# Softmax attention and a leaky-ReLU layer on one core: row 8 of batch 0 is loaded and attended later, batch 1's q comes in two loads

## The chip, the cores and the metric

The kernel runs on one core of a Trainium2 chip. The metric is the device time of one execution in microseconds (us). TensorE is called PE, VectorE DVE, ScalarE ACT, GpSimd POOL and SyncE SP, as in the profile. Each has its own queue of instructions, which it works off in order; data that one engine makes for another is handed over by semaphores.

## The reference

Inputs are q, k, v of 8 batches x 8 heads x 576 rows x 64, and two weight matrices, all fp32. Per head, q is softmaxed along its 64 columns and k along its 576 rows; then q times (k transposed times v). The result, 4608 tokens of 512, goes through two matrix products with a leaky ReLU between them.

```python
q_s = softmax(q, axis=-1)
k_s = softmax(k, axis=2)
kv = np.einsum('bhsd,bhse->bhde', k_s, v)
x = np.einsum('bhsd,bhde->bhse', q_s, kv)      # then to (4608, 512)
h = x @ w_in                                    # w_in: 512 x 2048
out = np.maximum(0.01 * h, h) @ w_out           # w_out: 2048 x 512
```

## The kernel before

The schedule is written out by hand: the order in which the program emits instructions is the order of each engine's queue. A framework adds semaphores and gives out buffers: a tile taken from a pool whose buffers are all in use waits until an older one is released.

A batch lies in SBUF as 128 partitions x 4 head pairs x 9 rows x 64 columns. A "row" r of a batch below means one of these nine, 64 tokens of each head. The output of attention for all batches is xT (bf16, transposed), and the two layers run over it in nine tiles of 512 tokens. Since a batch has 576 tokens, tile 0 is batch 0's rows 0 to 7, and tile 1 is batch 0's row 8 and batch 1's rows 0 to 6.

Attention of some rows takes these steps. `load` (L80, SP) fetches q, k or v. For q: `q_max` (L214, DVE), `q_sub` (L273, POOL or DVE), `q_exp` (L281, ACT), `q_sum` (L290 and L292, DVE), `q_norm` (L297, DVE), `q_transpose` (L402, PE, into PSUM) and `q_keep` (L417 or L419, a copy out of PSUM). For k: `k_tree` (L150), `k_allmax` (L155 to L175), `k_sub` (L183), `k_exp` (L191, ACT). `v_cast` (L201 on ACT, L203 on POOL) makes bf16 of v. `kv` (L310, PE) multiplies k and v into two PSUM tiles, `kd_make` (L329, L330) divides by k's sums, `cross` (L429, PE) applies q, and `x_keep` (L452, L454) copies the result to xT. Batch 0 has special forms of some steps (`q_first`, `kv_pair`, `k_max_pe`).

PSUM has two pools: psB with six buffers of 2 KB per partition and psO with two. In layer 2 of tile 0 (L499) the four accumulators `pout` take the two of psO and two of psB.

Tile 0 is cut into halves of 256 tokens. For half 0, layer 1 (`begin`, `end_pe`, L478) runs in two groups of eight column blocks, J0 and J1, and between its passes it does attention work of batch 0 (`x1`, `t2`, `x2`). Then comes half 1, and then layer 2 in 16 steps of four matmuls. J1 needs the second half of w_in.

Work of batch 1 hangs on hooks: `at(t, u, ...)` places functions at point u of tile t, and `run(t, u)` emits them. In tile 0, points 16 to 31 follow the 16 blocks of half 1 (two at a time, after the leaky ReLU of a pair), and point 32 + j follows step j of layer 2. So point 41 comes after 40 layer-2 matmuls, and point 45 after 56.

Loads go through two queues. SP's queue carries q, k, v and the stores; POOL's carries the weights, which it casts to bf16 on the way (`load_w_in`, `load_w_out`). `hold_sync` makes SP wait: the first one waits for a block of w_in's second half, and behind it SP issues batch 1's k in two parts, q's rows 0 to 6, and v. The second one, in `late_loads`, waits for a block of w_out and is followed by the rest of batch 1's q and by batch 2. POOL waits in the same way for the last block of w_in (L601) before it issues w_out's other blocks.

Of the kernel before, what the change touches and what calls it, by code (L numbers as in the profile page):

```python
# [8 lines left out]
FP32 = mybir.dt.float32  # L9
# [10 lines left out]
L = 64  # L20
# [5 lines left out]
def kernel(  # L26
# [9 lines left out]
    nc = tc.nc  # L36
# [10 lines left out]
    P = 128  # L47
    NB = C // P
    NF = F // P
    TT = 512  # L50
# [18 lines left out]
    BANK_TAG = "bank2k"  # L69


    def load(src, b, name, cuts, t=None):

        if t is None:
            t = raw_pool.tile([P, HL, R, D], FP32, name=name, tag="raw")
        flat = src[b].rearrange("h s d -> (h s d)").rearrange(
            "(hl p r d) -> p hl r d", hl=HL, p=P, r=R
        )
        for hs, rs in cuts:
            nc.sync.dma_start(  # L80
                out=t[:, hs, rs].rearrange("p h r d -> p h (r d)"),
                in_=flat[:, hs, rs].rearrange("p h r d -> p h (r d)"),
            )
        return t

    ALLH, ALLR = slice(0, HL), slice(0, R)
# [5 lines left out]
    st[0]["q"] = load(q, 0, "q_raw", [(ALLH, RA)])  # L92
    st[0]["k"] = load(k, 0, "k_raw", [(slice(0, 2), ALLR), (slice(2, 4), ALLR)])
    st[0]["v"] = load(v, 0, "v_raw", [(slice(0, 2), ALLR), (slice(2, 4), ALLR)])
    load(q, 0, "q_raw", [(ALLH, RB)], st[0]["q"])

    zero = const_pool.tile([P, TT], BF16)
    nc.gpsimd.memset(zero, 0.0)  # L98
# [91 lines left out]
    def k_exp(b, hs):  # L190
        nc.scalar.activation(  # L191
            out=st[b]["ke"][:, :, hs].rearrange("p r h d -> p h r d"),
            in_=st[b]["k"][:, hs],
            func=AF.Exp,
        )

    def v_cast(eng, b, gg):
        o = vb2[b % 2][:, :, gg, :, 0:D].rearrange("p r h d -> p h r d")
        i = st[b]["v"][:, 2 * gg : 2 * gg + 2]
        if eng is nc.scalar:  # L200
            eng.copy(out=o, in_=i)  # L201
        else:
            eng.tensor_copy(out=o, in_=i)  # L203
# [7 lines left out]
    def q_max(b, rs):  # L211
        n = rs.stop - rs.start
        st[b]["qmax", rs.start] = m = small_pool.tile([P, HL, n], FP32, name="qmax")
        nc.vector.tensor_reduce(out=m, in_=st[b]["q"][:, :, rs], axis=AX.X, op=ALU.max)  # L214
# [55 lines left out]
    def q_sub(eng, b, rs):  # L270
        n = rs.stop - rs.start
        qs = st[b]["q"][:, :, rs]
        eng.tensor_tensor(  # L273
            out=qs,
            in0=qs,
            in1=st[b]["qmax", rs.start].unsqueeze(3).to_broadcast([P, HL, n, D]),
            op=ALU.subtract,
        )
# [119 lines left out]
    def q_transpose(b, r0, n, pool=psB_pool, tag=BANK_TAG):  # L398
        ps = pool.tile([P, NB, n, L], BF16, name="psum_qt", tag=tag)
        for rr in range(n):  # L400
            for gg in range(2):
                nc.tensor.matmul(  # L402
                    ps[:, gg::2, rr],
                    lhsT=st[b]["qe"][:, r0 + rr, 2 * gg : 2 * gg + 2].rearrange(
                        "p h d -> p (h d)"
                    ),
                    rhs=ident,
                    is_transpose=True,
                    start=(rr == 0 and gg == 0),
                    stop=(rr == n - 1 and gg == 1),  # L410
                )
        st[b]["ps", r0] = ps

    def q_keep(eng, b, r0, n, gs=slice(0, 4)):
        o, i = st[b]["qT"][:, gs, r0 : r0 + n], st[b]["ps", r0][:, gs]
        if eng is nc.scalar:
            eng.copy(out=o, in_=i)  # L417
        else:
            eng.tensor_copy(out=o, in_=i)  # L419
# [44 lines left out]
    def attend_all(b, *parts):  # L464
        for fn in sum([attend_rows(b, *p) for p in parts], []):
            fn()

    def q_turn(b, rs=ALLR):
        if rs.start == 0:
            st[b]["qX"] = qT_pool.tile([P, R * 2, P], BF16, name="qX", tag="qT")  # L470
        nc.sync.dma_start_transpose(
            out=st[b]["qX"][:, 2 * rs.start : 2 * rs.stop],
            in_=st[b]["qe"][:, rs].rearrange("p r h d -> p (r h d)"),
        )
# [35 lines left out]
    def at(t, u, *fns):  # L510
        while t > 0 and u >= 32:
            t, u = t + 1, u - 32
        hooks.setdefault((t, u), []).extend(fns)
# [15 lines left out]
    def hold_sync(i, src):  # L529
        nc.sync.dma_start(out=held[:, i], in_=src)  # L530
# [59 lines left out]


    hold_sync(0, w_in_sb[0:1, 0, F - 128 : F])
    st[1]["k"] = load(k, 1, "k_raw", [(H0, ALLR), (H1, ALLR)])
    RM, RE = slice(4, 7), slice(7, R)
    st[1]["q"] = load(q, 1, "q_raw", [(ALLH, slice(0, 7))])
    st[1]["v"] = load(v, 1, "v_raw", [(ALLH, ALLR)])

    def late_loads():
        q_max(0, R3)
        q_sub(nc.gpsimd, 0, R3)  # L600
        nc.gpsimd.tensor_copy(out=gate[:, 0:1], in_=w_in_sb[:, NB - 1, F - 1 : F])  # L601
        for j0, j1 in ((2, 4), (4, 6), (6, 8), (8, 10), (10, 12), (12, 16)):
            load_w_out(slice(j0, j1))
        hold_sync(1, w_out_sb[0:1, 11, 0:128])
        load(q, 1, "q_raw", [(ALLH, RE)], st[1]["q"])
        load_all(2)


    at(0, 22, lambda: q_transpose(0, 8, 1), lambda: q_keep(nc.scalar, 0, 8, 1))
    at(0, 26, lambda: attend_all(0, (R3, (nc.scalar, nc.vector))))  # L610
    at(0, 20, lambda: k_begin(1), lambda: q_begin(1), lambda: k_tree(1, H0), lambda: k_tree(1, H1))
    at(0, 20, lambda: q_max(1, RA), lambda: q_sub(nc.gpsimd, 1, RA), lambda: k_allmax(1))
    at(0, 20, lambda: k_sub(nc.vector, 1, H1), lambda: k_sub(nc.gpsimd, 1, H0))
    at(0, 20, lambda: q_max(1, RM), lambda: q_sub(nc.gpsimd, 1, RM), lambda: v_cast(nc.gpsimd, 1, 1))
    at(0, 31, lambda: q_exp(1, RA), lambda: q_sum(1, RA), lambda: q_norm(1, RA))
    at(0, 31, lambda: k_exp(1, H1), lambda: v_cast(nc.scalar, 1, 0), lambda: k_exp(1, H0))
    at(0, 32, lambda: q_exp(1, RM), lambda: q_sum(1, RM), lambda: q_norm(1, RM))
    for r0 in (0, 2):
        at(0, 41, lambda r0=r0: q_transpose(1, r0, 2), lambda r0=r0: q_keep(nc.scalar, 1, r0, 2))
    at(0, 41, lambda: kv(1), lambda: kd_make(1))  # L620
    at(0, 44, lambda: q_transpose(1, 4, 3), lambda: q_keep(nc.scalar, 1, 4, 3))
    at(0, 45, lambda: attend_all(1, (slice(0, 7), (nc.scalar, nc.vector))))
    at(0, 46, lambda: q_max(1, RE), lambda: q_sub(nc.gpsimd, 1, RE), lambda: q_exp(1, RE))
    at(1, 14, lambda: q_sum(1, RE), lambda: q_norm(1, RE))
    at(1, 25, lambda: q_transpose(1, 7, 2), lambda: q_keep(nc.scalar, 1, 7, 2))
# [63 lines left out]
    def end_act(j, ph, half):  # L689
# [4 lines left out]
    t2 = (  # L694
        lambda: q_transpose(0, 6, 2, psO_pool, "pout"),
        lambda: q_keep(nc.vector, 0, 6, 2),
        lambda: q_sum(0, R3),
    )
    x2 = (
        lambda: attend_all(0, (slice(4, 8), (nc.scalar, nc.vector))),  # L700
        lambda: q_norm(0, R3),
    )
    x1 = (
        lambda: attend(0, (1,), RA),
# [6 lines left out]
    begun = list(zip(J0, begin(J0, ((0, x1), (1, ()), (2, ())))))  # L711
    for j, ph in begun:
        end_pe(j, ph, 0, slice(3, 4), False)
    for i, (j, ph) in enumerate(begun):
        end_act(j, ph, 0)
        if i == 0:
            q_sum(0, R1)
            q_norm(0, R1)
            q_exp(0, R2)
            late_loads()  # L720
            q_sum(0, R2)
            q_norm(0, R2)
        if i == 1:
            q_transpose(0, 4, 2, psO_pool, "pout")
            q_keep(nc.scalar, 0, 4, 2)
    q_exp(0, R3)
    for j, ph in zip(J1, begin(J1, ((0, t2), (1, x2), (2, ())))):
        end_pe(j, ph, 0, slice(3, 4), False)
        end_act(j, ph, 0)
# [69 lines left out]
```

## Time and profile before

| | us |
|---|---|
| median of 3 runs | 285.56 (285.51 to 285.58) |
| the profiled execution | 285.4 |
| its span in the profile | 283.6 |
| PE busy | 275.2 (97%) |
| ACT busy | 146.1 (52%) |
| DVE busy | 141.5 (50%) |
| POOL busy | 89.7 (32%) |
| DMA, mean over the span | 162 GB/s |

Times inside the execution count from the start of the span. A line of a timeline has the start, the duration, the engine, the source line, the operation with its tiles and shapes, and how many instructions are merged into it; in brackets is the idle time of the engine before it, and what ended that. A line of the waits has who waited for whom, the total, how often, and the longest. A line on DMA issues ends with the size and the time from issue to landing.

### The profile page before, as it was taken

The numbers are of one execution on the slowest core, as the hardware profiler recorded it, in microseconds if no ns is written. First come the engines' busy times: TensorE is split into PE (matmuls) and PEld (weight loads), VectorE is DVE, ScalarE is ACT, GpSimd is POOL, SyncE is SP. The second block draws the span as 40 slices with busy tenths as digits, with TensorE's granted clock in tenths as the row PEclk, the third lists the DMA queues.
The fourth block names the chain that finished last, engine by engine and source line by source line (L and its number), as shares of the span: only waits on it lengthen the run. The fifth ranks groups of instructions, "written<-read, shape, count | busy, mean of one in ns | idle before, by whom it ended". The sixth has DMA issues, their size and how long they took to land.

```text
span 283.6 us, 4991 instructions
## 1 busy us (share of the span) xinstructions
PE 275.2 (97%) x2022; PEld 132.8 (47%) x2022; DVE 141.5 (50%) x237; ACT 146.1 (52%) x260; POOL 89.7 (32%) x63
## 2 busy tenths in 40 slices
PE   7789999999999999999999999999999999999995
PEld 3368644444444544444444444444444444444443
DVE  2975695977870993497093718481711100110011
ACT  4976573775359426921973367435843165016400
POOL 2956390035069019407800690059000000000000
PEclk9999999999999999999999999999999999999999
DMA  7999999894659175953498339832052210230033
GB/s 239 334 211 341 281 177 395 265 352 159 152 122 404 51 161 132 408 121 75 102 401 158 74 80 378 201 76 63 11 86 55 61 34 0 55 82 14 0 74 76
DMA packets 37143, 45.81 MB, mean 162 GB/s; under 512 B 16000, under 2 KB 20352, under 8 KB 37120
## 3 DMA queue, kind: packets, MB, share of 16 engines
q1 hardware_dynamic: 33648, 41.16, 48.9%
q0 software_dynamic: 3312, 4.20, 8.4%
q8 instruction: 16, 0.26, 0.4%
q10 hardware_dynamic: 160, 0.13, 0.1%
q14 instruction: 7, 0.06, 0.1%
HBM read 36.70 MB, written 9.44 MB: 163 GB/s over the span
## 4 chain that ended last, share of the span: by engine, by line
PE 77%; DMA 8%; DVE 8%; POOL 3%; issue 1%; SPq 1%; ACT 0%; DVEq 0%; POOLq 0%
PE pout L499 39%; PE ph L478 34%; DMA q_raw<-in_q_dram 3%; DMA w_in_sb<-in_moe_w_in_dram 3%; DMA k_raw<-in_k_dram 2%; PE pkv L310 2%; PE po L429 2%; DVE qmax L214 2%; DVE k_raw L183 1%; POOL q_raw L273 1%; DVE out_sb L493 1%; DVE qe L297 1%; DVE t L150 1%; POOL w_in_sb L123 1%; SPq L80 1%
## 5 line engine op out<-in xcount | busy, mean ns | idle before, releaser
L499 PE MATMUL pout<-w_out_sb,gj 128*128 128x512 bf16 (+2 forms) x592 | 128.1, 373 | 0.0
L478 PE MATMUL ph<-xT,w_in_sb 128*128 128x512 bf16 (+1 forms) x640 | 127.4, 358 | 0.7 <-DMA w_in_sb<-in_moe_w_in_dram 0.7
L487 ACT ACTIVATE gj<-ph 128x512 bf16<-128x512 f32 x144 | 81.7, 602 | 54.1 <-PE ph L478 53.5
L478 PEld LDWEIGHTS <-w_in_sb 128*128 128x128 bf16 x640 | 61.9, 98 | 62.3 <-DMA w_in_sb<-in_moe_w_in_dram 0.8
L499 PEld LDWEIGHTS <-gj 128*128 128x128 bf16 x592 | 56.2, 98 | 65.2 <-ACT gj L487 0.7
L493 DVE COPY out_sb<-pout 128x512 f32<-128x512 f32 (+1 forms) x34 | 22.7, 676 | 88.2 <-PE pout L499 82.7
L183 POOL TENSOR_TENSOR k_raw<-k_raw,kall 128x2304 f32<-128x2304 f32 (+1 forms) x6 | 29.1, 4857 | 75.6 <-DVE kall L175 62.1
L452 ACT CAST xT<-po 128x512 bf16<-128x512 f32 (+4 forms) x46 | 18.2, 486 | 43.6 <-PE po L429 43.6
L273 POOL TENSOR_TENSOR q_raw<-q_raw,qmax 128x2304 f32<-128x2304 f32 (+5 forms) x13 | 31.6, 2431 | 24.3 <-DVE qmax L214 23.6
L290 DVE TENSOR_REDUCE qsum<-qe 128x36 f32<-128x2304 bf16 (+5 forms) x13 | 20.1, 1544 | 33.0 <-ACT qe L281 33.0
L297 DVE TENSOR_TENSOR qe<-qe,qrec 128x2304 bf16<-128x2304 bf16 (+5 forms) x13 | 21.5, 1650 | 0.4
L214 DVE TENSOR_REDUCE qmax<-q_raw 128x36 f32<-128x2304 f32 (+5 forms) x13 | 19.9, 1538 | 1.9 <-DMA q_raw<-in_q_dram 1.9
L191 ACT ACTIVATE ke<-k_raw 128x2304 bf16<-128x2304 f32 (+2 forms) x11 | 17.6, 1603 | 5.8 <-POOL k_raw L183 4.5
L281 ACT ACTIVATE qe<-q_raw 128x2304 bf16<-128x2304 f32 (+5 forms) x13 | 17.2, 1324 | 4.7 <-POOL q_raw L273 4.7
L203 POOL CAST vb<-v_raw 128x1152 bf16<-128x1152 f32 x14 | 16.8, 1223 | 0.0
L150 DVE TENSOR_TENSOR t<-k_raw 128x1024 f32<-128x1024 f32 (+1 forms) x10 | 10.1, 1006 | 2.1 <-DMA k_raw<-in_k_dram 1.9
L150 DVE TENSOR_TENSOR t<-t 128x256 f32<-128x256 f32 (+2 forms) x20 | 9.6, 478 | 0.6
L493 ACT COPY out_sb<-pout 128x512 f32<-128x512 f32 (+1 forms) x3 | 1.6, 549 | 15.1 <-PE pout L499 15.1
L341 PE MATMUL pout<-zero 128*128 128x512 bf16 x24 | 7.6, 453 | 1.3 <-POOL zero L98 1.3
L310 PEld LDWEIGHTS <-ke 64*64 64x64 bf16 x576 | 5.8, 106 | 3.2 <-ACT gj L487 1.7
L228 ACT ACTIVATE qe<-q_raw,nmax 128x64 bf16<-128x64 f32 x16 | 5.3, 333 | 3.4 <-DVE nmax L223 3.4
L310 PE MATMUL pkv<-vb,ke 64*64 64x65 bf16 x576 | 6.8, 194 | 0.2
(56 smaller groups left out, 89.0 us busy)
## 6 DMA issues: line engine op xcount, KB each, us to landing
out_dram<-out_sb SPq DMA_DIRECT2D x70, 128.0 KB, 2.4
v_raw<-in_v_dram SPq DMA_DIRECT2D x7, 1152.0 KB, 11.3
k_raw<-in_k_dram SPq DMA_DIRECT2D x6, 1152.0 KB, 5.8
q_raw<-in_q_dram SPq DMA_DIRECT2D x6, 1152.0 KB, 8.1
k_raw<-in_k_dram SPq DMA_DIRECT2D x4, 576.0 KB, 5.6
w_in_sb<-in_moe_w_in_dram POOLq DMA_DIRECT2D x8, 256.0 KB, 7.7
w_out_sb<-in_moe_w_out_dram POOLq DMA_DIRECT2D x6, 256.0 KB, 11.3
v_raw<-in_v_dram SPq DMA_DIRECT2D x2, 576.0 KB, 7.4
```

Of the source, the lines that this page charges most:

```text
L150: nc.vector.tensor_tensor(out=o, in0=i0, in1=i1, op=ALU.max)
L183: eng.tensor_tensor(out=ks, in0=ks, in1=st[b]["kall"][:, hs].unsqueeze(2).to_broadcast([P, n, R, D]), op=ALU.subtract,)
L214: nc.vector.tensor_reduce(out=m, in_=st[b]["q"][:, :, rs], axis=AX.X, op=ALU.max)
L273: eng.tensor_tensor(out=qs, in0=qs, in1=st[b]["qmax", rs.start].unsqueeze(3).to_broadcast([P, HL, n, D]), op=ALU.subtract,)
L290: nc.vector.reduce_sum(out=qsum, in_=st[b]["qe"][:, rs], axis=AX.X)
L297: eng.tensor_tensor(out=qes, in0=qes, in1=st[b]["qrec", rs.start].unsqueeze(3).to_broadcast([P, n, HL, D]), op=ALU.mult,)
L310: nc.tensor.matmul(outs[hh][hp * D : (hp + 1) * D, 0 : D + 1], lhsT=st[b]["ke"][rows, r, 2 * gg + hp], rhs=vb2[b % 2][rows, r, gg, hp, 0 : ...
L452: eng.copy(out=o, in_=ps)
L478: nc.tensor.matmul(ph, lhsT=w_in_sb[:, cb, j * P : (j + 1) * P], rhs=xT[:, cb, c0 : c0 + n], start=(cb == 0 and first), stop=(cb == NB - 1 ...
L487: nc.scalar.activation(out=o, in_=ph, func=AF.Prelu, alpha=LEAKY_SLOPE)
L493: copy(out=out_sb, in_=pout)
L499: nc.tensor.matmul(pout, lhsT=g_sb[j // 2][:, j % 2, tsub * P : (tsub + 1) * P], rhs=w_out_sb[:, j, os], start=(j == 0), stop=(j == NF - 1),)
```

## The change

- Batch 0's second q load takes rows 4 to 7 instead of 4 to 8. Row 8 gets a load of its own, on SP behind the first `hold_sync` and ahead of batch 1's k.
- Batch 1's rows 0 to 6 of q come in two loads, rows 0 to 3 and rows 4 to 6, instead of one.
- Row 8's maximum, subtraction (now on DVE) and exp move from tile 0's half 0 to point 19, its sum and norm to point 32, its transpose to point 42.
- Batch 1's transposes of rows 0 to 3, its `kv` and `kd_make` move from point 41 to point 42, with row 8's transpose between them.
- A new function `attend_next` at point 46 applies row 8 and batch 1's rows 0 to 6 into four shared PSUM tiles of 512 columns, and copies each out in one piece. Row 8's own attention at point 26, and batch 1's at point 45, are gone.
- Sum and norm of rows 4 and 5 and the exp of rows 6 and 7 are emitted ahead of the first leaky ReLU instead of behind it.

```diff
-    load(q, 0, "q_raw", [(ALLH, RB)], st[0]["q"])
+    load(q, 0, "q_raw", [(ALLH, slice(4, 8))], st[0]["q"])
...
+    def attend_next():
+        for gg in range(2):
+            ps = [psB_pool.tile([P, TT], FP32, name="po", tag=BANK_TAG) for _ in range(2)]
+            cross(0, gg, [a[:, 0:L] for a in ps], R3)
+            cross(1, gg, [a[:, L:TT] for a in ps], slice(0, 7))
+            st[1]["next", gg] = ps
+        for gg in range(2):
+            for hp, eng in ((0, nc.scalar.copy), (1, nc.vector.tensor_copy)):
+                eng(out=xT[:, 2 * gg + hp, TT : 2 * TT], in_=st[1]["next", gg][hp])
...
     hold_sync(0, w_in_sb[0:1, 0, F - 128 : F])
+    load(q, 0, "q_raw", [(ALLH, R3)], st[0]["q"])
     st[1]["k"] = load(k, 1, "k_raw", [(H0, ALLR), (H1, ALLR)])
     RM, RE = slice(4, 7), slice(7, R)
-    st[1]["q"] = load(q, 1, "q_raw", [(ALLH, slice(0, 7))])
+    st[1]["q"] = load(q, 1, "q_raw", [(ALLH, RA), (ALLH, RM)])
     st[1]["v"] = load(v, 1, "v_raw", [(ALLH, ALLR)])
 
     def late_loads():
-        q_max(0, R3)
-        q_sub(nc.gpsimd, 0, R3)
...
-    at(0, 22, lambda: q_transpose(0, 8, 1), lambda: q_keep(nc.scalar, 0, 8, 1))
-    at(0, 26, lambda: attend_all(0, (R3, (nc.scalar, nc.vector))))
+    at(0, 19, lambda: q_max(0, R3), lambda: q_sub(nc.vector, 0, R3), lambda: q_exp(0, R3))
...
+    at(0, 32, lambda: q_sum(0, R3), lambda: q_norm(0, R3))
     at(0, 32, lambda: q_exp(1, RM), lambda: q_sum(1, RM), lambda: q_norm(1, RM))
-    for r0 in (0, 2):
-        at(0, 41, lambda r0=r0: q_transpose(1, r0, 2), lambda r0=r0: q_keep(nc.scalar, 1, r0, 2))
-    at(0, 41, lambda: kv(1), lambda: kd_make(1))
+    for bb, r0, n in ((1, 0, 2), (1, 2, 2), (0, 8, 1)):
+        at(0, 42, lambda bb=bb, r0=r0, n=n: q_transpose(bb, r0, n), lambda bb=bb, r0=r0, n=n: q_keep(nc.scalar, bb, r0, n))
+    at(0, 42, lambda: kv(1), lambda: kd_make(1))
     at(0, 44, lambda: q_transpose(1, 4, 3), lambda: q_keep(nc.scalar, 1, 4, 3))
-    at(0, 45, lambda: attend_all(1, (slice(0, 7), (nc.scalar, nc.vector))))
+    at(0, 46, lambda: attend_next())
...
     t2 = (
         lambda: q_transpose(0, 6, 2, psO_pool, "pout"),
         lambda: q_keep(nc.vector, 0, 6, 2),
-        lambda: q_sum(0, R3),
     )
     x2 = (
         lambda: attend_all(0, (slice(4, 8), (nc.scalar, nc.vector))),
-        lambda: q_norm(0, R3),
     )
...
+    q_sum(0, R1)
+    q_norm(0, R1)
+    q_exp(0, R2)
     for i, (j, ph) in enumerate(begun):
         end_act(j, ph, 0)
         if i == 0:
-            q_sum(0, R1)
-            q_norm(0, R1)
-            q_exp(0, R2)
             late_loads()
...
-    q_exp(0, R3)
```

## The prediction

> **What bounds the kernel now.** I read the page first, then the waits of PE, then each engine's timeline from 14 to 50 us, and last the DMA queues in short windows. The page says that PE is the bound:
>
> ```profile
> PE 275.2 (97%) x2022; PEld 132.8 (47%) x2022; DVE 141.5 (50%) x237; ACT 146.1 (52%) x260; POOL 89.7 (32%) x63
> ...
> PE   7789999999999999999999999999999999999995
> ```
>
> Only PE's lost time counts. All edits lie before tile 1 starts on PE, and from there PE is full, so I forecast when tile 1 starts; the rest moves along with it. PE's waits after the start-up are small:
>
> ```profile
> PE psum_qt L402 <- DVE qe L297: 0.8, 2, 0.6
> ...
> PE ph L478 <- DMA w_in_sb<-in_moe_w_in_dram: 0.7, 1, 0.7
> ```
>
> The timeline of PE places them: 0.67 us before 20.17 (w_in), 0.17 us before 21.38 (rows 6 and 7 not normalised), 0.65 us before 41.53 (batch 1's rows not normalised). Tile 1 starts at 49.08:
>
> ```profile
> 32.08 8.80 PE L499 MATMUL pout<-w_out_sb,gj 128*128 128x512 bf16 x40
> 41.53 0.61 PE L402 MATMUL psum_qt<-ident,qe 128*128 128x128 bf16 x8 [0.65 <-DVE qe L297]
> 42.06 0.85 PE L310 MATMUL pkv<-vb,ke 64*64 64x65 bf16 x72
> ...
> 49.08 13.98 PE L478 MATMUL ph<-xT,w_in_sb 128*128 128x512 bf16 x64
> ```
>
> ACT's timeline shows what stands in front of that kv, in program order: half of k, the cast of v, the other half of k, rows 4 to 6 of q, then the copies of the transposes:
>
> ```profile
> 36.41 1.16 ACT L191 ACTIVATE ke<-k_raw 128x1152 bf16<-128x1152 f32 x1 [0.53 <-DVE k_raw L183]
> 37.48 1.14 ACT L201 CAST vb<-v_raw 128x1152 bf16<-128x1152 f32 x1
> 38.90 1.16 ACT L191 ACTIVATE ke<-k_raw 128x1152 bf16<-128x1152 f32 x1 [0.29 <-POOL k_raw L183]
> 40.33 0.84 ACT L281 ACTIVATE qe<-q_raw 128x768 bf16<-128x768 f32 x1 [0.27 <-POOL q_raw L273]
> 41.95 1.07 ACT L417 COPY qT<-psum_qt 128x512 bf16<-128x512 bf16 x2 [0.78 <-PE psum_qt L402]
> ```
>
> Batch 1's v is issued last on SP (22.45) and its issue row reads 14.8 us to landing: 37.25, so the cast at 37.48 has no slack. DMA is the tight resource. Below are the queue rows of three windows, 26.2 to 27.4 us, 29 to 34 us and 37.5 to 40 us, and v's issue row. Columns are packets, MB and share of the 16 engines; q1 carries SP's loads, q0 the weights.
>
> ```profile
> q1 hardware_dynamic: 268, 0.48, 104.3%
> ...
> q1 hardware_dynamic: 458, 1.02, 58.7%
> q0 software_dynamic: 472, 0.45, 53.4%
> ...
> q0 software_dynamic: 521, 0.52, 124.1%
> ...
> v_raw<-in_v_dram SPq DMA_DIRECT2D x1, 1152.0 KB, 14.8
> ```
>
> From 29 to 34 us the two queues take turns, one packet for one (458 to 472), though q1's carry more bytes. A q1 packet here is one row: 128 partitions x 4 heads = 512 rows per load, 32 per engine. Prices: w_out alone 16 x 2.5 us / 521 = 77 ns; a q row of 1792 B alone 16 x 1.2 / 268 = 72 ns; in turns, v's 32 rows on the slowest engine fill 31.49 (q lands) to 37.25, so 180 ns a pair; v's row alone is 92 ns (347 rows, 0.80 MB, from 24 to 26 us), so w_out's turn takes 88.
>
> **The change, part by part.** *Rows 4 to 7 in the first q load.* 131 KB less in front of w_in. By bytes at the 391 GB/s of 10 to 11.2 us that is 0.33 us, by packets (still 512) nothing; I take 0.3, since the 1280-B row's 52 ns there against 72 for 1792 B says that bytes count. PE's w_in wait shrinks to about 0.35.
>
> *Rows 6 and 7 sooner.* ACT's exp (0.62) moves ahead of the first leaky, and row 8's max (0.41), sum (0.41), reciprocal (0.18) and norm (0.42) leave DVE's queue here, its subtraction (0.61) POOL's. The norm that ended at 21.3 is done about 0.65 sooner. The leaky goes 0.2 later, covered by the w_in wait. Gain 0.17, between 0 (if w_in isn't sooner) and 0.17.
>
> *Row 8 moved behind.* Two transposes (28.18 to 28.29) and eight small matmuls (30.13 to 30.32) leave PE here, 0.30, and come back later. The layer-2 matmuls then start at 32.08 - 0.3 - 0.17 - 0.30 = 31.3. Row 8's new max, sub and exp at hook 19 find DVE idle (24.1 to 26.0) and ACT with 0.2 to 0.3 us between leakys; they cost nothing unless row 8 lands after about 26. Its sum and norm, 0.41 + 0.18 + 0.42, now stand on DVE before batch 1's rows 4 to 6.
>
> *Row 8's load.* One SP issue more (0.5 us) before k, and 512 rows of 256 B. No row shows such a load; by bytes 0.33 us, at the 27 ns of the 512-B rows (361 packets from 42.1 to 42.7 us) 0.85. I take 0.55, nearer to the latter's kind; k's second half lands at 27.46 - 0.3 + 0.55 = 27.7. [...]
>
> *Batch 1's q in two loads.* Same bytes but 1024 rows instead of 512, 32 more turns per engine. Before, the slowest engine spent 27.46 to 31.49 on 32 rows, n at 72 ns alone and the rest at 72 + 88: n = 12.4, so 0.9 us alone before w_out came in. After, k is 0.25 later and w_out 0.3 sooner (POOL's gate waits for w_in): 0.35 us alone. Row prices between 27 ns (512 B) and 72 (1792 B): 44 for 1024 B, 36 for 768 B. So 8 rows alone and 24 x (44 + 88) = 3.2: rows 0 to 3 land at 31.2, hardly sooner than the 31.49 of before, though they are four sevenths of the bytes. Rows 4 to 6: 32 x (36 + 88) = 4.0, to 35.2. v: 32 x 180 = 5.8, to 41.0, that is 3.7 us later than now. Ends: 40.1 (w_out no sooner, a cheap row-8 load) and 42.0 (no row alone, a dear one). w_out has turns left: of its 112 rows per engine (14 blocks of 128 over 16) the slowest has used some 88 by then.
>
> *The norm chain.* The max of rows 0 to 3 starts 0.25 sooner, and DVE's 0.28 copy of row 8 is gone: their norm ends near 41.0 instead of 41.39, row 8's near 42.1. PE reaches hook 42 at 31.3 + 44 x 0.22 = 41.0. Hook 41 to 42 hides what was the 0.65 wait, but row 8's transposes wait about 0.7.
>
> *What is queued behind v.* On ACT: cast 1.14, k's other half 1.16, rows 4 to 6's exp 0.84, then the first transposes' copy 0.59 (a 128x512 copy at 20.02). Less overlaps of about 0.1 each, 3.65. kv needs k's other half. It also needs a bank: layer 2 holds two of the six of that pool, three transposes take three, kv's two tiles want five where four are left, so its second tile waits for that copy. (Two transposes left room before.) kv starts at 41.0 + 3.65 = 44.65 instead of 42.06. POOL's cast of v (2.14 from 41.0) is done by then, so are the norm and kd_make, which are needed later.
>
> *One stretch.* Attending row 8 and rows 0 to 6 together takes 16 matmuls; four copies of 512 columns (0.58, 0.69) replace six. Only four layer-2 matmuls (0.87) cover them now, instead of eight. Copies of the first pair end about 0.7 after their matmuls, and tile 1 needs the second pair 0.43 after the first: between 0 and 0.3; I take 0, as in the 1.9 us of cover before.
>
> *The sum.* Before, kv's start to tile 1 is 0.79 + 6.23, with 24 layer-2 matmuls after kv. Now there are 20 (-0.86) and eight more small ones (+0.19): 0.79 + 5.56. Tile 1 starts at 44.65 + 6.35 = 51.0, against 49.08: 1.9 us later. The profiled execution took 285.4 us, span 283.6 and 1.8 around it; 287.3. The median of the runs shown is 0.16 above it, so 287.4 to 287.5. Forecast 287.4.
>
> **Rivals.** *The turns hold more than one small row (not slower).* If queues shared by bytes, rows of 1024 and 768 B would pay 39 and 29 ns for w_out instead of 88: rows 0 to 3 land at 27.7 + 0.35 + 24 x 0.083 = 30.0, rows 4 to 6 at 32.1, v at 37.9. ACT's chain ends before PE is there. PE can't come much sooner either: w_out's third block, issued near 25.2 with 12 us to landing, comes at 37.2, and its first matmul now runs at 32.08 + 24 x 0.22 = 37.4. So hook 42 near 41.6, first copy done 42.45, kv at 42.5, tile 1 at 48.85: 0.2 gained, 0.7 if kv needn't wait for a bank. Time 285.0. This decides if v lands before 39.05, where tile 1 breaks even. For it: no row shows rows below 1792 B in turns with w_out. Against: two 1792-B rows to a turn would take at most 32 x 116 = 3.7 us after 27.46, and q took 4.03. [...]
>
> *kv doesn't wait for the copy.* If v is late but a bank is free, or the slowest engine lags less and v lands near 39.7, kv starts at 43.3: tile 1 is 0.55 late, 286.0.
>
> *PE slows after the pause.* Between 41.0 and 44.65 PE has only ten transposes. The first weight loads show a slow PE: 0.42 us apart from 1.72 to 4.28, then six in 1.20 us. Three us at that half pace again would cost 1.5: 288.9. [...] Against: the pauses of before, 0.8 us at most after the first matmuls, never show it.
>
> **How the numbers follow.** The forecast's case 0.58 (286.3 to 288.3), kv without the copy 0.13 (285.5 to 286.4), turns by bytes 0.16 (284.5 to 285.4), the slow PE 0.09 (288.3 to 289.5), others 0.04. The range 284.8 to 288.8 leaves out part of the third and most of the fourth. The forecast case alone: 286.3 to 288.3, from v at 40.1 to 42.0 and the copies' 0.3. Runs of this kernel can tell about 0.2%, 0.57 us. Faster 0.11 (most of the third case), same 0.15 (its rest, half of the second), slower 0.74.
>
> **What would show it.** v's issue row at 17 to 18 us to landing instead of 14.8; ACT's cast at 41.0 after an idle time put down to v's load; rows 0 to 3's load no shorter than 9 us; a wait of some 2.5 us on PE before kv at 44.65, put down to the copy or to k's exp; tile 1 at 51.0; w_in's wait at 0.35; three transposes before kv. If v lands by 39, the turns are wrong and so is the sign; if kv starts right after k's exp, the bank is; if matmuls after kv are 0.43 apart, the third rival holds.

## The result and the profile after

The changed kernel takes 288.66 us (median; 287.68 to 289.54), against 285.53 for the kernel before: a ratio of 1.0109, with a 95% interval from 1.0066 to 1.0152. It is 1.1% slower. Its executions come in two kinds, near 287.7 and near 289.5 with a mean granted clock of PE of 0.992, and the median lies between them; what the runs below win or lose is counted from the first kind. The profiled execution is one of the first kind: 287.68 us, span 285.9, so 2.28 us more than the profiled one of before. In the profile of the changed kernel, later source lines are ten higher than before (L478 is now L488, L499 is L509).

The page, busy time of each engine and the slices of PE:

```profile
PE 275.3 (96%) x2022; PEld 132.7 (46%) x2022; DVE 141.3 (49%) x237; ACT 145.4 (51%) x259; POOL 89.3 (31%) x62
...
PE   7799988998999999999999999999999999999994
```

PE is busy as long as before (275.3 against 275.2), so the new time is waiting. The view of PE's waits (total, how often, longest) names it:

```profile
PE pkv L310 <- ACT qT L417: 1.0, 1, 1.0
...
PE pout L509 <- ACT gj L497: 0.8, 1, 0.8
...
PE psum_qt L402 <- DVE qe L297: 0.3, 1, 0.3
```

The wait for w_in (0.7) is gone, and the one for the norm is 0.3 instead of 0.8. In their place stand waits of `kv` for ACT and one of layer 2 on ACT's leaky ReLU. PE's timeline places those of `kv`, and a new one for w_out:

```profile
31.09 7.38 PE L509 MATMUL pout<-w_out_sb,gj 128*128 128x512 bf16 x32
38.93 2.75 PE L509 MATMUL pout<-w_out_sb,gj 128*128 128x512 bf16 x12 [0.47 <-DMA w_out_sb<-in_moe_w_out_dram]
41.52 0.72 PE L402 MATMUL psum_qt<-ident,qe 128*128 128x128 bf16 x10
42.71 0.21 PE L310 MATMUL pkv<-vb,ke 64*64 64x65 bf16 x1 [0.48 <-ACT ke L191]
43.92 0.79 PE L310 MATMUL pkv<-vb,ke 64*64 64x65 bf16 x71 [0.99 <-ACT qT L417]
```

Layer 2 starts 0.99 us sooner (32.08 before). `kv` runs at 43.92 instead of 42.06. Its first matmul waits for k's exp; the other 71 wait another 0.99 for ACT's copy of the transposes, which gives the bank back. ACT's timeline shows the queue in front of it:

```profile
40.44 1.16 ACT L201 CAST vb<-v_raw 128x1152 bf16<-128x1152 f32 x1 [3.48 <-DMA v_raw<-in_v_dram]
41.50 1.16 ACT L191 ACTIVATE ke<-k_raw 128x1152 bf16<-128x1152 f32 x1
42.57 0.83 ACT L281 ACTIVATE qe<-q_raw 128x768 bf16<-128x768 f32 x1
43.30 1.33 ACT L417 COPY qT<-psum_qt 128x512 bf16<-128x512 bf16 x3
```

ACT stands idle for 3.48 us until v lands at 40.42, and everything behind the cast is late with it. v's issue row (18.7 us to landing instead of 14.8), and then the queues from 29 to 34 us (packets, MB, share):

```profile
v_raw<-in_v_dram SPq DMA_DIRECT2D x1, 1152.0 KB, 18.7
```

```profile
q0 software_dynamic: 533, 0.51, 60.5%
q1 hardware_dynamic: 539, 0.87, 53.8%
```

The two queues still take turns one packet for one (533 to 539), though q1's packets have shrunk: 0.87 MB in that window, 1.02 before.

**Where the 2.28 us are.** Tile 1 starts 0.89 us later than before. Tile 2 starts another 0.98 later, which nothing in the forecast had. PE's timeline of the changed kernel:

```profile
49.97 13.98 PE L488 MATMUL ph<-xT,w_in_sb 128*128 128x512 bf16 x64
63.78 3.19 PE L509 MATMUL pout<-w_out_sb,gj 128*128 128x512 bf16 x14
67.72 4.33 PE L509 MATMUL pout<-w_out_sb,gj 128*128 128x512 bf16 x18 [0.75 <-ACT gj L497]
...
80.52 1.67 PE L488 MATMUL ph<-xT,w_in_sb 128*128 128x512 bf16 x7
```

and of the kernel before, where layer 2 of tile 1 has no such gap:

```profile
62.89 7.29 PE L499 MATMUL pout<-w_out_sb,gj 128*128 128x512 bf16 x32
...
78.65 1.67 PE L478 MATMUL ph<-xT,w_in_sb 128*128 128x512 bf16 x7
```

From tile 1's start to tile 2's it was 29.57 us and is 30.55. From tile 2's start to the last matmul it is the same (201.6 us). The last 0.4 us lie behind the last matmul (3.4 us to the end of the span before, 3.8 after), where the same copies and stores run in both kernels. The other profiled executions have 3.6 to 3.8 us there, also two versions of the kernel before (3.56 with two loads of q, 3.76 with three), so they are not put down to the change.

The wait at 67.72 comes from DVE. Its timeline in the changed kernel:

```profile
49.02 1.29 DVE L476 CAST xT<-po 128x512 bf16<-128x512 f32 x2 [2.58 <-PE po L429]
...
50.82 2.47 DVE L503 COPY out_sb<-pout 128x512 f32<-128x512 f32 x4
```

and before:

```profile
47.29 1.16 DVE L454 CAST xT<-po 128x448 bf16<-128x448 f32 x2 [2.98 <-PE po L429]
...
48.95 2.47 DVE L493 COPY out_sb<-pout 128x512 f32<-128x512 f32 x4
```

The stretch now stands at point 46, so DVE copies xT 1.73 us later while tile 1 is only 0.89 later. All of batch 2's k and q work stands behind those copies on DVE, then on POOL (its subtraction at 62.90 instead of 61.03), then on ACT, where the leakys of tile 1 stand behind batch 2's exp (67.09 instead of 65.22). Every one of these is 1.87 us later (1.73, and the rest from DVE's longer copies), PE 0.89, and 1.87 - 0.89 = 0.98 is the loss: that chain had no slack at all. POOL's and ACT's lines in the changed kernel:

```profile
62.90 4.19 POOL L273 TENSOR_TENSOR q_raw<-q_raw,qmax 128x1536 f32<-128x1536 f32 x2 [10.87 <-DVE qmax L214]
...
67.09 1.06 ACT L497 ACTIVATE gj<-ph 128x512 bf16<-128x512 f32 x2
```

and before:

```profile
61.03 4.19 POOL L273 TENSOR_TENSOR q_raw<-q_raw,qmax 128x1536 f32<-128x1536 f32 x2 [10.87 <-DVE qmax L214]
...
65.22 1.06 ACT L487 ACTIVATE gj<-ph 128x512 bf16<-128x512 f32 x2
```

### The profile page after: what moved, and what is told of

Its sections match the earlier page's. It is cut to its first block, busy times and chain, and to the rows that moved or that the text cites. A ratio compares the mean times of both kernels' runs of the same rounds, so it can differ in the third digit from the quotient of the medians.

```text
span 285.9 us, 4994 instructions
## 1 busy us (share of the span) xinstructions
PE 275.3 (96%) x2022; PEld 132.7 (46%) x2022; DVE 141.3 (49%) x237; ACT 145.4 (51%) x259; POOL 89.3 (31%) x62
## 4 chain that ended last, share of the span: by engine, by line
PE 77%; DMA 11%; DVE 5%; POOL 2%; issue 2%; SPq 1%; ACT 1%; POOLq 0%; DVEq 0%; ACTq 0%
PE pout L509 39%; PE ph L488 34%; DMA v_raw<-in_v_dram 7%; DMA k_raw<-in_k_dram 2%; DMA w_in_sb<-in_moe_w_in_dram 2%; PE pkv L310 2%; PE po L429 2%; SPq L80 1%; POOL q_raw L273 1%; DVE out_sb L503 1%; DVE k_raw L183 1%; DVE t L150 1%; DVE qmax L214 1%; POOL w_in_sb L123 1%; DVE xT L476 0%
## 5 line engine op out<-in xcount | busy, mean ns | idle before, releaser
L509 PE MATMUL pout<-w_out_sb,gj 128*128 128x512 bf16 (+2 forms) x592 | 128.6, 373 | 1.5 <-ACT gj L497 0.8
L488 PE MATMUL ph<-xT,w_in_sb 128*128 128x512 bf16 (+1 forms) x640 | 127.2, 358 | 0.0
L488 PEld LDWEIGHTS <-w_in_sb 128*128 128x128 bf16 x640 | 62.0, 98 | 61.7 <-issue 0.2
L509 PEld LDWEIGHTS <-gj 128*128 128x128 bf16 x592 | 56.2, 98 | 67.0 <-ACT gj L497 1.6
L273 POOL TENSOR_TENSOR q_raw<-q_raw,qmax 128x2304 f32<-128x2304 f32 (+4 forms) x12 | 31.9, 2666 | 24.7 <-DVE qmax L214 24.0
L452 ACT CAST xT<-po 128x512 bf16<-128x512 f32 (+3 forms) x43 | 17.0, 488 | 43.1 <-PE po L429 43.1
L297 DVE TENSOR_TENSOR qe<-qe,qrec 128x2304 bf16<-128x2304 bf16 (+5 forms) x13 | 20.8, 1602 | 0.4
L203 POOL CAST vb<-v_raw 128x1152 bf16<-128x1152 f32 x14 | 16.0, 1168 | 0.0
```

The lines of the kernel that those rows point to most:

```text
L273: eng.tensor_tensor(out=qs, in0=qs, in1=st[b]["qmax", rs.start].unsqueeze(3).to_broadcast([P, HL, n, D]), op=ALU.subtract,)
L297: eng.tensor_tensor(out=qes, in0=qes, in1=st[b]["qrec", rs.start].unsqueeze(3).to_broadcast([P, n, HL, D]), op=ALU.mult,)
L488: nc.tensor.matmul(ph, lhsT=w_in_sb[:, cb, j * P : (j + 1) * P], rhs=xT[:, cb, c0 : c0 + n], start=(cb == 0 and first), stop=(cb == NB - 1 ...
L509: nc.tensor.matmul(pout, lhsT=g_sb[j // 2][:, j % 2, tsub * P : (tsub + 1) * P], rhs=w_out_sb[:, j, os], start=(j == 0), stop=(j == NF - 1),)
```

## The experiments

The theory: v's load is late because SP's rows take turns with w_out's rows one for one, `kv` waits behind v on ACT and then for a bank, and separately the stretch's place delays DVE. The rivals: the two loads cost by their number and not by their rows; `kv` is late for another reason than v; the late w_in or the clock decides; the whole is one loss and not two.

### One load for q

```diff
-    st[1]["q"] = load(q, 1, "q_raw", [(ALLH, RA), (ALLH, RM)])
+    st[1]["q"] = load(q, 1, "q_raw", [(ALLH, slice(0, 7))])
```

> The changed kernel, but batch 1's q rows 0 to 6 in one load again (512 rows of 1792 B instead of 1024 shorter ones). Theory of single-row turns: 32 turns per engine fewer in front of v. With k landing at 27.8 as in the changed kernel and some 0.55 us alone, q lands at 27.8 + 0.55 + 24 x 0.16 = 32.2 and v at 32.2 + 32 x 0.18 = 38.0 instead of 40.4. The norm chain of rows 0 to 3 starts 1.2 later (32.2 instead of 31.0), so k's half and the exp of rows 4 to 6 end near 42.5 by POOL's work, the first copy near 43.3, and kv starts near 43.4 instead of 43.9: 0.5 us faster than the changed kernel's fast profile. Rival, that v is late by the row-8 load or by one DMA more and not by the count of rows: v still lands after 40 and the time stays.

Measured: 287.23 us, ratio 1.0061 (1.0046 to 1.0076). v lands at 38.04, 2.4 us sooner than with two loads. But all seven rows of q now land at 32.4 instead of 30.9 for the first four, so the chain of q's rows comes later: the exp of rows 4 to 6 now waits for POOL, and `kv` runs at 43.60, only 0.3 sooner, still 0.64 behind the copy. PE's timeline of this kernel:

```profile
43.60 0.79 PE L310 MATMUL pkv<-vb,ke 64*64 64x65 bf16 x71 [0.64 <-ACT qT L417]
```

Tile 1 starts at 49.66. So the second load makes v late as forecast, but undoing it returns 0.45 us and not 1.9: what else the change moved behind `kv` holds it nearly as long.

### Two loads, but cut by heads

Rows stay 1792 B long and their number stays at 512; only the number of loads is two.

```diff
-    st[1]["q"] = load(q, 1, "q_raw", [(ALLH, RA), (ALLH, RM)])
+    st[1]["q"] = load(q, 1, "q_raw", [(H0, slice(0, 7)), (H1, slice(0, 7))])
```

> The changed kernel, but batch 1's q rows 0 to 6 split by heads instead of by rows: two loads of 256 rows of 1792 B, together as many rows as one load. If the count of rows sets v, v lands near 38.0 as with one load, and the second half of q near 32.2; time as with one load within 0.2 us. If a second load costs by itself, v lands near 40.4 and the time is that of the changed kernel.

Measured: 287.39 us, ratio 1.0068 (1.0053 to 1.0083). v's issue row in this kernel:

```profile
v_raw<-in_v_dram SPq DMA_DIRECT2D x1, 1152.0 KB, 15.2
```

It was issued at 22.87 and landed at 38.07, as with one load (38.04). So it is the number of rows that costs, not the number of loads. The time is that of one load, too.

### The kernel before with two loads

```diff
-    st[1]["q"] = load(q, 1, "q_raw", [(ALLH, slice(0, 7))])
+    st[1]["q"] = load(q, 1, "q_raw", [(ALLH, RA), (ALLH, RM)])
```

> The kernel before, with the one edit that batch 1's q comes in two loads (rows 0 to 3, rows 4 to 6). Single-row turns: k lands at 27.5 as before, 0.9 us alone passes 20 rows of 1024 B, 12 more in turns, rows 0 to 3 land at 30.0; rows 4 to 6 at 34.0; v at 39.7 instead of 37.25. The wait of 0.65 for the norm goes, but ACT's cast of v starts at 39.7, k's other half ends at 41.95, and kv starts near 42.0, as before (two transposes leave it a bank). So v 2.4 us later for no change of the time, 285.5 within 0.2%. Rival, that rows share by bytes: v at 38, the norm wait gone, 0.5 us faster.

Measured: 285.23 us over ten executions, ratio 0.9995 (0.9986 to 1.0005): no change. v lands at 40.1 instead of 37.25. ACT's cast of v starts at 40.17, after 3.48 us of idle time. PE's timeline of this kernel:

```profile
42.44 0.80 PE L310 MATMUL pkv<-vb,ke 64*64 64x65 bf16 x72 [1.09 <-ACT ke L191]
```

The late v is there in full, and so is the wait on ACT. But the 0.65 us wait for q's norm is gone, since rows 0 to 3 land sooner, and here all 72 matmuls of `kv` start together: there are only two transposes, and a bank is free. So the cut as a whole costs this kernel nothing measurable. That is a balance, and not slack: the late v still makes `kv` wait 1.09 us, and the sooner norm gives about as much back (the last experiment takes that wait away and is faster).

### Row 8's transpose out of the way

The transpose of row 8 goes to point 44, so that `kv`'s second tile finds a bank.

```diff
-    for bb, r0, n in ((1, 0, 2), (1, 2, 2), (0, 8, 1)):
+    for bb, r0, n in ((1, 0, 2), (1, 2, 2)):
...
+    at(0, 44, lambda: q_transpose(0, 8, 1), lambda: q_keep(nc.scalar, 0, 8, 1))
```

> The changed kernel, but row 8's transpose and its copy are moved from in front of kv to point 44, so that kv finds four free banks for two transposes and its own two tiles. If the bank was the last wait, kv starts when k's other half is exponentiated, 42.7, with no wait for the copy: 1.2 us sooner than 43.9; then the transposes of rows 4 to 6 wait some 0.4 for their norm, so 0.8 to 1.2 us faster than the changed kernel. If the bank isn't it, kv still starts near 43.9.

Measured: 287.10 us, ratio 1.0058 (1.0042 to 1.0075). PE's timeline of this kernel:

```profile
43.09 0.81 PE L310 MATMUL pkv<-vb,ke 64*64 64x65 bf16 x72 [1.33 <-ACT ke L191]
```

The wait for the copy is gone and `kv` comes 0.83 sooner although v is 0.4 later here (40.84); 0.23 is lost again three steps on, to the norm of rows 4 to 6. The bank is shown. It was worth some 0.55 us of the time, where 0.8 to 1.2 were expected.

### ACT's order: the cast of v last

```diff
-    at(0, 31, lambda: k_exp(1, H1), lambda: v_cast(nc.scalar, 1, 0), lambda: k_exp(1, H0))
+    at(0, 31, lambda: k_exp(1, H1), lambda: k_exp(1, H0), lambda: v_cast(nc.scalar, 1, 0))
```

> The changed kernel with one swap in ACT's order: both halves of k's exp before the cast of v instead of the cast between them. v still lands at 40.4. Theory of the queue behind v: k's second half no longer waits for v, so cast 40.4 to 41.6, exp of rows 4 to 6 to 42.4, first copy to 42.9: kv goes on at 42.9 or 43.0 instead of 43.9, 1.0 us sooner, 286.6 to 286.9 in executions of full clock. If v's lateness doesn't act through ACT's order, no change.

Measured: 287.08 us, ratio 1.0068 (1.0048 to 1.0088); the profiled execution 286.80. Two of the four are near 286.8, as expected, and two are longer (287.33 and 288.19). PE's timeline of this kernel:

```profile
43.01 0.79 PE L310 MATMUL pkv<-vb,ke 64*64 64x65 bf16 x71 [1.03 <-ACT qT L417]
...
66.81 4.33 PE L509 MATMUL pout<-w_out_sb,gj 128*128 128x512 bf16 x18 [0.75 <-ACT gj L497]
...
79.62 1.67 PE L488 MATMUL ph<-xT,w_in_sb 128*128 128x512 bf16 x7
```

k's exp no longer stands behind v, and `kv` is 0.9 us sooner, as expected. Tile 1 starts at 49.07, within 0.01 of the kernel before. Tile 2 starts at 79.62, 0.97 later than before. This shows best that there are two losses: with the first one made good in full, the second stands there unchanged, with its wait of 0.75.

### The stretch at point 45

```diff
-    at(0, 46, lambda: attend_next())
+    at(0, 45, lambda: attend_next())
```

> The changed kernel with the joint stretch (row 8 and batch 1's rows 0 to 6) at point 45 instead of 46, so with eight layer-2 matmuls behind it as the old one had. Theory: the second loss, the wait of 0.75 us on ACT near 67 us, comes from DVE: the copies of the stretch stand ahead of the stores' copies and batch 2's k in its queue, and at point 46 they start 1.7 us later than before while tile 1 starts only 0.9 later. At 45 the stretch waits some 0.15 for the copy of rows 4 to 6, tile 1 starts near 50.1, the copies 0.8 sooner, the wait near 67 shrinks to 0.2 or less: 0.6 to 0.8 us faster than the changed kernel's fast profile, 286.9 to 287.1. Rival, that the wait near 67 comes from the shape of the copies or from batch 2's late loads: no change, or 0.15 slower.

Measured: 286.98 us over ten executions, ratio 1.0053 (1.0021 to 1.0086). Two of the ten took 288.8 and 288.9, with a granted clock of 0.994; the others 286.5 to 287.3. PE's timeline of this kernel:

```profile
63.61 7.39 PE L509 MATMUL pout<-w_out_sb,gj 128*128 128x512 bf16 x32
...
79.48 2.75 PE L488 MATMUL ph<-xT,w_in_sb 128*128 128x512 bf16 x12
```

DVE's copies of xT start at 47.98, 1.04 sooner than at point 46, the wait in layer 2 is gone, and tile 1 to tile 2 takes 29.68 us, within 0.1 of before. Tile 1 itself starts at 49.80, 0.72 late, as `kv` runs at 43.68.

### Three parts undone together

The edits shown above for one load, for row 8's transpose at 44 and for the stretch at 45, all in the changed kernel. Row 8's own load and the sooner rows 6 and 7 remain.

> The changed kernel with three things undone: one load for batch 1's rows 0 to 6, row 8's transpose behind kv (point 44), the stretch at point 45. What stays is row 8's own load, its later work and the joint stretch. If the three losses are the row count in front of v, the bank and the stretch's place, this is the kernel before within 0.2%: kv near 42.3 with 44 layer-2 matmuls done, the transposes of rows 4 to 6 wait 0.5 for their norm, tile 1 near 49.0; 285.2 to 285.7. If something else in the row-8 move costs, 286.2 or more.

Measured: 286.10 us over ten executions, ratio 1.0014 (0.9987 to 1.0042). Most of the loss is gone, but it is some 0.5 us above what was expected. PE's and POOL's timelines of this kernel show a wait that neither kernel had:

```profile
43.54 0.48 PE L310 MATMUL pkv<-vb,ke 64*64 64x65 bf16 x36 [1.13 <-POOL vb L203]
```

```profile
39.74 2.45 POOL L273 TENSOR_TENSOR q_raw<-q_raw,qmax 128x768 f32<-128x768 f32 x1
42.14 1.34 POOL L203 CAST vb<-v_raw 128x1152 bf16<-128x1152 f32 x1
```

POOL's cast of v ends at 43.48 (42.39 before), and half of `kv` waits for it. It is late for two reasons. q lands at 32.4 instead of 31.49, behind row 8's load. And POOL's subtraction of rows 4 to 6 takes 2.45 us instead of 1.46, because DVE's norm now starts ahead of it (39.59 against 39.74; last section). The second weighs less than it seems, since the cast is shorter in return (1.34 us against 2.14): from the subtraction's start to the cast's end it is 3.74 us, and 3.56 before. So 0.91 of the 1.09 us come from the later q. Neither was undone by itself.

### Three loads of q

The kernel before, with rows 0 to 1, 2 to 3 and 4 to 6 in a load each: 512 rows more than in two loads.

```diff
-    st[1]["q"] = load(q, 1, "q_raw", [(ALLH, slice(0, 7))])
+    st[1]["q"] = load(q, 1, "q_raw", [(ALLH, slice(0, 2)), (ALLH, slice(2, 4)), (ALLH, RM)])
```

> The kernel before with batch 1's rows 0 to 6 of q in three loads (rows 0 and 1, 2 and 3, 4 to 6): 1536 rows in front of v instead of 512, the same bytes. Single-row turns: 0.9 us alone passes 33 rows of 512 B at 27 ns, 31 more at 27 + 88, rows 0 to 3 land at 31.9, rows 4 to 6 at 35.9, v at 41.7. Then the cast and k's other half end at 44.0 and kv starts there instead of 42.06: 1.9 us slower, 287.3. If rows shared by bytes, v lands at 38 and the time is 285.4.

Measured: 286.95 us over ten executions, ratio 1.0055 (1.0018 to 1.0091). v lands at 40.65, where 41.7 was expected: the third load made v 0.5 later than two loads did, where 1.6 was expected. From 28 to 29 us q1 moved 181 packets (0.14 MB) and q0 111, from 29 to 31 us 219 and 211: in the first of these windows 70 of q1's rows went without a row of w_out in turn. So not every row in front of v cost it a turn; the forecast had counted too many. Two of the ten executions, 288.77 and 288.93, have a granted clock of 0.993, though row 8 is where it was before; neither is the profiled one.

### The pause filled

The remaining question is the second kind of execution. The same changed kernel was run again.

> The changed kernel as it is, once more, so that the runs beside it share a chip with it. Expected: between 287.7 and 289.5 us, with the same chain: v at 40.4, kv's second matmul at 43.9 behind the first copy, tile 1 near 50.0, and 0.98 us more than before lost between tile 1's and tile 2's start.

Measured: 289.58, 291.76, 287.60 and 287.56 us, ratio 1.0109 (1.0019 to 1.0198). The clocks are 0.993, 0.992, 0.997 and 0.998. This time the profiled execution is the one of 289.58. PE's timeline, and the windows (stretch, its length, then PE, PEld, DVE, ACT and POOL busy with their instructions, PE's granted clock, DMA share, GB/s):

```profile
44.28 0.89 PE L310 MATMUL pkv<-vb,ke 64*64 64x65 bf16 x71 [0.99 <-ACT qT L417]
45.50 2.99 PE L509 MATMUL pout<-w_out_sb,gj 128*128 128x512 bf16 x7 [0.34 <-issue]
```

```profile
44.00:45.00 1.00, 0.72 (x71) 0.72 (x70) 0.96 (x2) 0.99 (x3) 0.00 (x0) 0.87 0.97 371
45.00:46.00 1.00, 0.67 (x15) 0.39 (x7) 0.97 (x3) 0.00 (x0) 0.00 (x0) 0.50 1.03 410
...
48.00:49.00 1.00, 1.00 (x10) 0.68 (x9) 0.00 (x0) 0.14 (x1) 0.00 (x0) 0.92 1.00 392
```

From about 44.74 to 48.16 (0.87 and 0.92 of a window, with the windows between at 0.50) the clock is half: 3.4 us. Seven matmuls of layer 2 that take 1.67 us elsewhere take 2.99. Tile 1 starts at 51.92, 1.95 later than in the other kind. The pause ahead of it, from the last matmul of layer 2 to the body of `kv`, is 41.4 to 44.28, and in it are ten transposes and one small matmul. In the profiled execution of the first kind the pause is 2.2 us long (41.68 to 43.92).

The traces' records of the clock show when it falls. Its changes here, at 7.20, 44.74, 48.16 and 287.09 us, lie whole multiples of 3.413 us apart, and in all fourteen traces full clock lasts a whole number of such steps (81 to 83 of them where nothing interrupts it). So the trace can be cut into these steps. In the fourteen traces every step at full clock in which PE is busy for 1.41 us or less is followed by half clock, and every one with 1.48 us or more by full clock. Most of the low ones are at the end, where PE runs out of work. The step of the pause here, and the lowest one that kept the clock (the kernel before with two loads, at its end):

```profile
41.33:44.74 3.41, 1.27 (x69) 0.99 (x69) 0.95 (x1) 3.41 (x6) 0.99 (x1) 1.00 0.77 217
```

```profile
279.08:282.49 3.41, 1.48 (x20) 1.10 (x18) 0.29 (x1) 0.48 (x1) 0.00 (x0) 1.00 0.59 143
```

In the profiled execution of the first kind PE is busy for at least 1.95 us in any 3.41 us around the pause. So, as far as one trace of the second kind can tell, an execution is of that kind when its pause is half a microsecond or more longer and its idle time falls within one step.

To tell the pause from other causes, 28 matmuls of zeros were put into `kv`'s first tile between the transposes and `kv`, where PE waits anyway; `kv` then overwrites them.

```diff
+        if b == 1:
+            for i in range(28):
+                nc.tensor.matmul(
+                    pkv[0].rearrange("p g d -> p (g d)"),
+                    lhsT=zero[:, 0:P],
+                    rhs=zero[:, 0 : 2 * (D + 2)],
+                    start=True,
+                    stop=True,
+                )
```

> The changed kernel with 28 matmuls of zeros (132 columns each, some 1.6 us) on PE between the transposes of point 42 and kv, into kv's first tile, which kv overwrites. Nothing else moves; they end before kv may go on. Theory: the executions at 289.5 us with a mean clock of 0.992 come from PE's pause before kv, after which it runs at half pace for 3.4 us in some executions. With the pause filled no execution shows a clock of 0.994 or less, and all lie between 287.4 and 288.0. Rival, that the slow executions have another cause: about half of them stay at 289.5.

Measured: 287.80 us (289.68, 287.80, 287.79, 289.98, 287.67, 287.50), ratio 1.0107 (1.0079 to 1.0135). No execution has a clock under 0.998, where the changed kernel had four of eight at 0.992 or 0.993. If half of the executions were to fall still, six at full clock in a row would have a chance of 1 in 64; and in the profiled one PE is busy for at least 2.35 us in any 3.41 us that begin between 30 and 52 us, far from 1.41. So the pause is what lets the clock fall. But two executions are near 289.8 all the same, at full clock: in the profiled one of these (289.68) v lands at 42.43, w_out's blocks make PE wait three times (0.54, 0.37, 0.69), and `kv` comes at 45.91.

```profile
43.09 1.77 PE L323 MATMUL pkv<-zero 128*128 128x132 bf16 x28
45.91 0.79 PE L310 MATMUL pkv<-vb,ke 64*64 64x65 bf16 x71 [0.89 <-ACT qT L426]
```

So there is another cause of long executions, transfers that lag by 1 to 2 us in the same place; what makes them lag no run shows. The zeros cost nothing: the other four are where the changed kernel is at full clock. Among the executions of the kernel before, one took 289.08 us at a clock of 0.993; the changed kernel's 291.76 has something more than the clock that no trace shows.

### Two versions made of what was found

The kernel before with two loads of q and the cast of v last (the two edits shown above):

> The kernel before with two edits: batch 1's q in two loads, and the same swap on ACT. In the run with the split alone the norm no longer waited, and kv waited 1.09 us for k's second half behind the cast. With the swap that half is done near 39.1, the cast near 41.3, POOL's cast near 41.5, and kv starts near 41.4 right behind the transposes: tile 1 at 48.3 instead of 49.1, 0.6 to 0.8 us faster than the kernel before, 284.6 to 284.8. If kv then waits for something that the trace didn't show, 285.4.

Measured: 284.43 us (six executions at 284.35 to 284.57, and 286.24 in the profiled one), ratio 0.9968 (0.9956 to 0.998). It is 0.3% faster than the kernel before, a little more than expected, and so faster than both. The profiled execution was the one with late transfers, SP's wait for w_in ending 0.7 later than before, so the gain is not seen in a trace. What it does show is that `kv` follows the transposes, which start at 42.23, with no wait:

```profile
42.77 0.81 PE L310 MATMUL pkv<-vb,ke 64*64 64x65 bf16 x72
```

The changed kernel with the cast last, row 8's transpose at 44 and the stretch at 45:

> The changed kernel with the swap on ACT, row 8's transpose behind kv (point 44) and the stretch at point 45; the two loads stay. kv waits for neither k nor a bank, and starts at 42.1 to 42.3 with 44 layer-2 matmuls done (the wait of 0.47 for w_out stays); tile 1 at 48.3 to 48.6 and no wait near 67 us: 284.7 to 285.0, 0.5 faster than the kernel before. If the wait for w_out or POOL's cast of v grows, 285.4 to 286.

Measured: 285.53 us over twelve executions (284.83 to 288.0), ratio 1.0017 (0.9998 to 1.0037); 284.7 to 285.0 was expected. One of the twelve, the 288.0, has a clock of 0.994. The mends bring the changed kernel back to the kernel before, not below it. Its profiled execution, 287.54, again had late transfers (v at 42.8, PE waiting 0.45 and 0.85 for w_out), so why the others stay half a microsecond above the expectation is open.

## Why the prediction was right, and where not

The sign held, and so did the mechanism of the first half of the loss. The size came out by luck, twice: two errors cancel (below), and the median, 288.66, lies inside the range up to 288.8 only because the four executions fell two and two into kinds near 287.8 and 289.5. In the forecast's order:

- *Turns of one row for one.* v was put at 41.0 and landed at 40.42; rows 0 to 3 at 31.2 and 30.9, rows 4 to 6 at 35.2 and 34.8, k at 27.7 and 27.78. The window counts (533 to 539), one load (38.04) and the cut by heads (38.07) show that rows count, and neither bytes nor loads. The rival by bytes, the one on the other side, asked for v at 37.9 and falls. That the rows go singly, and not several of one queue in a run, shows in windows as short as a row in the kernel before: from 33.00 to 33.09 us the 16 engines start 10 rows of v and 6 of w_out, from 33.09 to 33.18 it is 6 and 10. In these turns the smaller rows lose their share: from 29 to 34 us q1 moved 0.87 MB in 539 packets here, and 1.02 MB in 458 before.
- *The queue behind v.* Cast, half of k, exp and copy: from the cast's start to `kv` 3.48 us, forecast 3.65. The forecast's own terms, 1.14 + 1.16 + 0.84 + 0.59 less three overlaps of 0.1, are 3.43, so its sum was wrong and its terms were right. The missing bank was right, and the rival without it falls (0.99 us for the copy; gone with the transpose moved).
- *The norm chain: rows 0 to 3 done near 41.0, row 8 near 42.1.* Measured 39.33 and 40.95. With the 0.28 us copy of row 8 gone from DVE, the norm starts just ahead of POOL's subtraction and no longer just behind it, and takes 1.25 us instead of 2.50 (last section). I had carried the 2.50 over. It won nothing, since `kv` stood behind v.
- *w_in's wait at 0.35.* Wrong: there was none. But the kernel before with two loads has none either, while two kernels with the shorter load wait 0.54 and 0.57. SP's wait for w_in ended at 18.34 here and between 18.36 and 20.84 in the other runs. This term changes from execution to execution by more than the edit's 0.3.
- *Rows 6 and 7 sooner, 0 to 0.17.* Mis-sized. With w_in early, PE waits 0.82 us for their norm in the kernels without this edit, and 0.29 in those with it: 0.53. Together with the row 8 work moved away, layer 2 starts at 31.09 (forecast 31.3).
- *Layer 2 runs on from there.* It does not: it now overtakes w_out and waits 0.47 at 38.93 (1.06 with one load). This takes back half of the 0.99 that the first steps had won.
- *`kv` at 44.65 and 6.35 from there to tile 1.* Measured 43.92 and 6.05. v was 0.6 sooner, and row 8's part of the attention adds 0.06 to it, not 0.19. So tile 1 was 0.89 late and not 1.9: this term was mis-sized by 1.0.
- *"All edits lie before tile 1 ... the rest moves along with it", and the stretch at 0.* This is the step that failed. The stretch cost tile 1 nothing, as taken, but its later copies on DVE pushed batch 2's work, which has no slack, and 0.98 us were lost near 67 us. The forecast had looked for the stretch's cost only at the next consumer of xT and not at what stands behind the copies on DVE. By 80.5 us the two errors add up to the forecast's number: 0.89 + 0.98 = 1.87 against 1.9. That the sum agrees is chance.
- *PE slows after the pause, chance 0.09.* It was forecast at 288.9 with 3 us at half pace, and it happens in four of the eight executions of the changed kernel, with 3.4 us at half pace and 289.5 us. No run shows the 3 us: it was my estimate, beside the 2.56 us (1.72 to 4.28) in which the first weight loads of before are 0.42 us apart; the trace shows 3.42 (44.74 to 48.16) in its place. The mechanism and price were about right, the chance far too low; it decides that the median is 288.66 and not 287.7. The argument against it, that the pauses of before never show it, was read from one profiled execution with shorter pauses. The clock that the trace shows in the slow stretch is 0.50, and its steps of 3.413 us start at 7.20 us there, at 4.29 in the kernel before and at 4.21 in the changed kernel's first trace. One step is longer than the whole pause of 2.9 us, and the longest stretch without any matmul in the pause is 1.15 us: PE was not idle for the whole step, and 1.27 us of work in it did not hold the clock.

## What to carry to other kernels

When a step is moved on an engine that is not the bound, follow everything behind it on that engine's queue until it meets the bound again, beyond the next consumer: a chain over engines that are busy a third to a half of the time can still have no slack (here POOL at 31%, DVE at 49% and ACT at 51%, and 0.98 us lost). Cutting a load into shorter rows can cost the loads behind it while another queue is busy: here 512 rows more put v at 40.42 instead of 38.04, and two loads with rows of the old length left it at 38.07. So cut by rows of the same length if it must be cut. When a wait is made longer on a PE that is otherwise full, ask whether its clock survives it (here 1.41 us of work in a step of 3.41 did not keep it up, and 1.48 did), and look at several executions and not one.

## What the runs showed that was not expected

- v's issue on SP took longer with more rows of q issued just ahead of it: 2.57 us in the changed kernel, and 1.39 to 2.28 in the other runs with 1024 rows; 0.53 before, 0.51 with one load of q and 0.47 with two cut by heads, all three with 512 rows. The three loads of q took 3.54 us to issue. What holds SP there no run shows. v's landing did not come from this: the issue had ended at 24.32, and its rows stood behind those of q, which landed at 34.8.
- DVE's norm of rows 0 to 3 and POOL's subtraction of rows 4 to 6 start within 0.15 us of each other, and only the one that starts first keeps its time (1.25 to 1.27 us on DVE, 1.46 to 1.47 on POOL). In the kernel before, POOL starts 0.05 us ahead, and DVE's norm takes 2.50 us. DVE's timeline, then POOL's:

```profile
38.88 2.50 DVE L297 TENSOR_TENSOR qe<-qe,qrec 128x1024 bf16<-128x1024 bf16 x1
```

```profile
38.83 1.46 POOL L273 TENSOR_TENSOR q_raw<-q_raw,qmax 128x768 f32<-128x768 f32 x1
```

  In the changed kernel DVE is 0.13 us ahead, and POOL's subtraction takes 2.45. The same two timelines:

```profile
38.08 1.25 DVE L297 TENSOR_TENSOR qe<-qe,qrec 128x1024 bf16<-128x1024 bf16 x1
```

```profile
38.21 2.45 POOL L273 TENSOR_TENSOR q_raw<-q_raw,qmax 128x768 f32<-128x768 f32 x1
```

  All runs that keep row 8's copy on DVE ahead of this are of the first kind (2.48 to 2.50 on DVE), all that have moved it of the second (2.45 to 2.46 on POOL). What holds the later one no run shows. So taking 0.28 us off DVE's queue made POOL's subtraction 1.0 us longer. The cast behind it on POOL is 0.8 us shorter in return (1.34 against 2.14), so who waits for the subtraction (ACT's exp with one load, 1.25 us) has 1.0 us more to wait, and who waits for the cast 0.2.
- A kernel's profiled execution can be one with late transfers: the two kernels of the last experiment took 286.24 and 287.54 us in it, against medians of 284.43 and 285.53. A reading from a single trace is good for the mechanism, and the medians are for the size.
